# A first unit with a corrected plan: the first load in two halves, its transposes split with it, and the weight-sum stores tied to another event

## The chip, the cores and the metric

The kernel runs on one NeuronCore of a Trainium2 chip. The metric is the device time of one execution in microseconds (us); lower is better. The time of the kernel before is the median of three executions, and one more execution was profiled. All times in this document are in us unless they are marked ns.

## The reference

Six cross layers of a recommender network over a batch of 16384 rows of 1024 bf16 features. Each layer multiplies the running activation by a 1024x1024 weight matrix, adds a bias, multiplies element by element with the original input and adds the running activation:

```python
def reference(x0, ws, bs):          # x0: [16384, 1024]  ws: [6, 1024, 1024]  bs: [6, 1024]
    x = x0
    for l in range(6):
        proj = jnp.einsum('bd,de->be', x, ws[l]) + bs[l]
        x = x0 * proj + x
    return x
```

## The kernel before, in words

**Tiling.** The batch is cut into 16 pairs of 1024 rows (`PR`), and a unit is one pair in one layer, so there are 96 units. Two neighbouring pairs form a group and take turns: layer 0 of the first, layer 0 of the second, layer 1 of the first, and so on. The activations lie transposed in SBUF (features on the partitions): `x0T` holds the input of a pair and `xst` its running activation.

**Products.** A unit's matrix product is done by a Strassen-like scheme on 2x2 blocks. Seven block products, named 1 to 7, are formed from four input blocks, four combinations of input blocks (`T1` to `T4`, made on DVE) and eight weight blocks: four raw ones (`w12`, `1`, `2`, `4`) and four sums (`5`, `6`, `7`, `3`, made on DVE while the first pair passes, by the operations `c5`, `c6`, `c7`, `c3`). `P1.m` means product 1 for output block m: four matmuls of 128x512 (line 394). Most units carry the scheme one level deeper for some products (`5p1`, `2p3` and so on, line 588: four matmuls of 128x256); these need quarter sums of weights, which DVE writes into a third `xst` buffer. The very first unit uses no inner level: it is 28 groups `Pi.m` of four matmuls, and the transposes described next.

**PSUM.** There are eight banks, `pA0` to `pA3` and `pX0` to `pX3`. ACT copies a bank to another (`F1.m`, `F.m`) so that two products can go on from the same partial sum, and moves finished sums with their bias to SBUF (`E2.m`, `E4.m`, ...).

**The order.** All instructions are written out before the launch, one static order for each engine; engines wait for each other only through semaphores. The order of TensorE's work is a list of names written by hand for each kind of unit (`PE_FIRST` for the first). The orders of DVE, ACT, POOL and SP come from a planner (`schedule`), a list scheduler that knows an occupation (`occ`) and a latency (`lat`) for each operation and, for the start, a table `ARRIVE` of times at which loads are taken to have landed. The planner's start times also place the later weight loads on SP's queue (`plan_loads`, `pump`, line 315). A wrong entry in `ARRIVE` harms nothing by itself, but it can place an operation behind another one that in fact is ready later.

**The start.** DVE clears a tile, TensorE does eight dummy matmuls on it (line 770) and SP issues the loads in this order: `load_rows(0)`, 512 KB of x0 in row order (line 786); the weight block `1` (line 789); `load_rows(1)` and `load_rows(2)`; the weight block `2` (line 792); `w12` and `4` in halves (line 779); one block of x0 by a transposing DMA (line 796); and the four blocks of the second pair by transposing DMAs (line 418). The three blocks `rows[0..2]` are transposed by TensorE: the operation `ti.k` is four 128x128 matmuls against an identity (line 498) into one bank, which `ui.k` casts into `x0T` (line 502: k = 0, 2 on ACT, k = 1, 3 on DVE). `bT` transposes the bias (line 509), and two small DVE operations keep it.

**Stores of the weight sums.** The eight sums of a layer (four blocks, four tiles of quarter sums) are stored to DRAM from POOL's queue for the later groups (`save`, line 445, 512 KB each). In the first unit they stand behind `gate@0`, a one-column copy on POOL (line 722), which reads a block of `xst` that DVE writes by the operation `Qm`.

Of the kernel before, what the change touches and what calls it, by code (L numbers as in the profile page):

```python
# [14 lines left out]
IDENT = mybir.ActivationFunctionType.Identity  # L15

PE_FIRST = """
t0.0 t0.2 t0.3 t0.1 P1.2 t1.0 t1.1 P1.0 bT t1.3 t1.2 t2.0 t2.1 P2.0 t2.2 P1.1 t2.3 P2.1 P1.3 P2.2 P5.0 P5.1 P5.2 P2.3 P6.0 P6.3 P6.2 P5.3 P7.0 P6.1 P7.2 P3.0 P7.3 P4.2 P7.1 P3.3 P3.1 P4.1 P3.2 P4.3 P4.0
""".split()
PE_ONE_INNER = """  # L20
P1.1 P1.0 P1.3 P1.2 P2.1 P6.1 P2.0 P6.2 5p5 5p1 P2.2 P6.0 5p6 5p2 P6.3 P2.3 5p7 5p3 P7.2 P7.3 P3.3 5p4 P3.1 P7.1 P4.3
# [19 lines left out]
P1.1 P1.0 P6.1 P1.3 P1.2 P2.1 P2.0 P2.3 P6.2 P2.2 P5.3 P6.3 P5.2 P6.0 P5.1 P5.0 P3.3 P3.2 P3.1 P3.0 P7.0 P7.1 P7.3  # L41
P7.2 P4.0 P4.3 P4.1 P4.2 tV.1 tV.0 xW.1 xW.3 xW.0 tW.1 xW.2 tW.3 tW.2 tV.3 tV.2 tW.0
""".split()
ARRIVE = {"rows0": 5.0, "w0.1": 6.4, "rows1": 8.1, "rows2": 9.6, "w0.2": 11.1, "h0": 13.0, "h1": 14.6, "q": 16.6, "next": 20.6, "raw1": 34.2, "sums": 13.5}


ACCUM = (9.5, 12.0, 9.0)
# [144 lines left out]
def kernel(  # L192
# [7 lines left out]
    nc = tc.nc  # L200
    P = nc.NUM_PARTITIONS
# [3 lines left out]
    KH = KD // 2  # L205
    H = D // 2
    NB = 512
# [4 lines left out]
    KQ, HQ, NQ = KH // 2, H // 2, NB // 2  # L212
# [22 lines left out]
    P1s, P5s, Q, U, V, W, C3 = (work.tile([P, KH, KH, P], BF16, name=f"ev{i}") for i in range(7))  # L235
# [94 lines left out]
        return wt[(gl, w)]  # L330

    ops, named = [], {}
    FAR = 1e9

    def at_home(r):
        p, dot, m = r.partition(".")
        return home[p] + dot + m if p in home else r

    def op(name, eng, occ, lat, fn, rd=(), wr=(), weights=(), key=None, after=(), due=FAR, at=0.0):
        rd, wr = [at_home(r) for r in rd], [at_home(r) for r in wr]  # L340
        rd = tuple(rd) + tuple(slot[k] for k in weights if k in slot)
        for k in weights:
            uses_left[k] = uses_left.get(k, 0) + 1
        named[name] = len(ops)
        ops.append(Op(name, eng, occ, lat, fn, rd, tuple(wr), tuple(weights), key, tuple(named[a] for a in after), due, at))

    QD = ((0, 0), (0, 1), (1, 0), (1, 1))
    for u, (pr, l) in enumerate(units):
# [12 lines left out]
        x0T, xst = x0Ts[pr % 3], xsts[pr % 3]  # L361
# [10 lines left out]
        def pe(name, occ, fn, rd, wr, weights=(), u=u, gl=gl, line=line, at=0.0):  # L372
            op(f"{name}@{u}", "PE", occ, occ + 0.19, fn, rd, wr, [(gl, w) for w in weights], key=(u, line[name]), at=at)

        def act(name, fn, rd, wr, biased_=False, u=u, early=0.0):
            occ = 0.583 if biased_ else 0.482
            op(f"{name}@{u}", "ACT", occ, occ + 0.17 - early, fn, rd, wr)

        def dve(name, fn, n, rd, wr, weights=(), u=u, gl=gl, at=0.0, due=FAR, early=0.0):
            occ = n / 1920 + 0.068  # L380
            op(f"{name}@{u}", "DVE", occ, occ + 0.12 - early, fn, rd, wr, [(gl, w) for w in weights], at=at, due=due)
# [33 lines left out]
        def load(pt, q, at=0.0, after=(), u=u):  # L415
            def fn():
                r0 = pt * PR + q[1] * NB
                nc.sync.dma_start_transpose(out=blk(x0Ts[pt % 3], *q), in_=x0[r0:r0 + NB, q[0] * H:(q[0] + 1) * H])
            op(f"ld{q[0]}{q[1]}.{pt}@{u}", "SP", 3.0, 8.0, fn, [], [f"x0.{pt % 3}.{q[0]}{q[1]}"], at=at, after=after)

        def let(q, sp, u=u, xst=xst, grp=grp):
            def fn():
# [17 lines left out]
        if grp == 0 and lane == 0:  # L440
            raw = lambda w, gl=gl: wt[(gl, w)]

            def save(w, t, rd, weights=(), l=l, u=u, gl=gl):
                def fn():
                    nc.gpsimd.dma_start(Lc[l, CIDX[w]].rearrange("p (k e) -> p k e", k=KH), t())
                op(f"s{w}@{u}", "POOL", 1.0, 7.0, fn, rd + (["gate"] if u == 0 else []), (), [(gl, x) for x in weights])

            if first:
                ga = const.tile([P, 1], BF16, name="gate")

            def combo(w, a, b, o_, deps, gl=gl, raw=raw, first=first):
                def part(sl):
                    tt(raw(w)[:, :, sl], raw(a)[:, :, sl], raw(b)[:, :, sl], o_)

                def fn():
                    ring_make(gl, w)
                    part(slice(0, HQ) if w == "5" and first else slice(0, H))
                rd = [f"w{gl}.{d}" for d in deps]
                if w == "5" and first:
                    dve("c5", fn, KH * HQ, ["ringmake"], ["w0.5a", "ringmake", slot[gl, w]], [a, b], at=ARRIVE["h0"])  # L460
                    dve("c5b", lambda part=part: part(slice(HQ, H)), KH * HQ, ["w0.5a"], ["w0.5"], [a, b], at=ARRIVE["h1"])
                else:
                    dve("c" + w, fn, KH * H, rd + ["ringmake"], [f"w{gl}.{w}", "ringmake", slot[gl, w]], [a, b], at=ARRIVE["raw1"] if gl == 1 else 0.0)
            combo("5", "w12", "4", ADD, ())
            combo("6", "5", "1", SUB, ("5",))
            combo("7", "1", "w12", SUB, ())
            combo("3", "2", "6", SUB, ("6",))
            for Xi in ISLOT:
                if Xi == "4i" and l not in K4:
                    continue  # L470
                X = Xi[0]
                a = lambda r, c, X=X, gl=gl: wt[(gl, X)][:, r * KQ:(r + 1) * KQ, c * HQ:(c + 1) * HQ]
                sv = isum(Xi).rearrange("p q (k e) -> p q k e", k=KQ)
                src = [] if X == "2" else [f"w{gl}.{5 if X == '4' else X}"]
                nm = lambda i, Xi=Xi: f"is.{Xi}.{i}"

                def icombo(i, fn, rd, Xi=Xi, X=X, src=src, nm=nm):
                    dve(Xi + i, fn, KQ * HQ, [nm(r) for r in rd] + src, [nm(i), ISN[Xi]], [X], at=ARRIVE["sums"] if first else 0.0)
                icombo("5", lambda a=a, sv=sv: tt(sv[:, 0], a(0, 1), a(1, 1), ADD), ())
                icombo("6", lambda a=a, sv=sv: tt(sv[:, 1], sv[:, 0], a(0, 0), SUB), "5")  # L480
                icombo("3", lambda a=a, sv=sv: tt(sv[:, 2], a(1, 0), sv[:, 1], SUB), "6")
                icombo("7", lambda a=a, sv=sv: tt(sv[:, 3], a(0, 0), a(0, 1), SUB), ())
# [8 lines left out]
        if first:  # L491
            for i, (d, n) in enumerate(TURNED):
                for k in range(KH):
                    xb = k if i < 2 else 2 + k % 2

                    def turn(i=i, k=k, xb=xb):
                        for j in range(KH):
                            nc.tensor.matmul(pX[xb][:, j * P:(j + 1) * P], lhsT=rows[i][:, j, k, :], rhs=ident[:],  # L498
                                             start=(j == 0), stop=True, skip_group_check=True)
                    pe(f"t{i}.{k}", 0.25, turn, [], [Xn[xb]], at=ARRIVE[f"rows{i}"])  # L500
                    cp = nc.vector.tensor_copy if k % 2 else nc.scalar.copy
                    f = lambda cp=cp, d=d, n=n, k=k, xb=xb, x0T=x0T: cp(out=blk(x0T, d, n)[:, k], in_=pX[xb][:])  # L502
                    if k % 2:
                        dve(f"u{i}.{k}", f, 1024, [Xn[xb]], [Xn[xb], X0[d, n]], early=0.21 * k if i < 2 else 0.0)
                    else:
                        act(f"u{i}.{k}", f, [Xn[xb]], [Xn[xb], X0[d, n]], early=0.21 * k if i < 2 else 0.0)

            def turn_bias():
                nc.tensor.matmul(pA[KH - 1][:, 0:LK], lhsT=b_rows[:], rhs=ident[0:LK, 0:LK], start=True, stop=True, skip_group_check=True)
                nc.vector.tensor_scalar_add(b_all[:, 0:KD], pA[KH - 1][:, 0:KD], 1.0)  # L510
                nc.vector.tensor_copy(out=b_all[:, KD:LK], in_=pA[KH - 1][:, KD:LK])
            pe("bT", 0.1, turn_bias, [], [A[KH - 1], "bias"])
        ttop("T1", Tv[1], B12, B11, SUB, [XI[0, 1], XI[0, 0]], ["T1"])
        ttop("T2", Tv[2], B22, Tv[1], SUB, [XI[1, 1], "T1"], ["T2"], at=ARRIVE["q"] if first else 0.0)
        ttop("T3", Tv[3], B22, B12, SUB, [XI[1, 1], XI[0, 1]], ["T3"], at=ARRIVE["q"] if first else 0.0)
# [203 lines left out]

        if grp == 0 and lane == 0:  # L720
            if first:
                op("gate@0", "POOL", 0.1, 0.3, lambda ga=ga, xst=xst: nc.gpsimd.tensor_copy(ga[:], xst[:, 0, 0, 0, 0, 0:1]), [XO[0, 0]], ["gate"])
            for w in MADE:
                save(w, lambda w=w, gl=gl: wt[(gl, w)], [f"w{gl}.{w}"], [w])
            for Xi in ISLOT:
                if Xi == "4i" and l not in K4:
                    continue
                save(Xi, lambda Xi=Xi: isum(Xi), [f"is.{Xi}.{i}" for i in "5637"] + [ISN[Xi]])
# [52 lines left out]
    take(4)  # L781
    nc.scalar.dma_start(b_rows[:], bs.rearrange("l (m p) -> (l m) p", p=P))

    def load_rows(i):
        d, n = TURNED[i]
        nc.sync.dma_start(rows[i][:].rearrange("p j m r -> p j (m r)"), x0[n * NB:(n + 1) * NB, d * H:(d + 1) * H].rearrange("(j p) d -> p j d", p=P))

    load_rows(0)
    nc.sync.dma_start(wt[(0, "1")][:], w_src(0, "1"))
    load_rows(1)  # L790
    load_rows(2)
# [46 lines left out]
```

## Time and profile before

| | |
|---|---|
| median of 3 executions | 2209.33 (2209.17 to 2209.70) |
| profiled execution, its own time | 2209.77 |
| its span, first to last instruction | 2208.0 |
| PE busy | 2194.8 (99%), 14878 instructions |
| DVE busy | 2149.9 (97%) |
| ACT busy | 2055.4 (93%) |
| POOL busy | 255.1 (12%) |
| DMA | 512.30 MB, mean 232 GB/s |

PE is TensorE's matmul side and PEld its weight loads, DVE is VectorE, ACT is ScalarE, POOL is GpSimd, SP is SyncE; a "q" behind an engine's name marks its sequencer, which issues DMAs. The span is 1.8 shorter than the same execution's time, and that execution is 0.44 over the median. In a timeline line, the first number is when a run of like instructions starts, the second how long it lasts, and the bracket at its end tells how long the engine had been idle and who released it.

### The profile page before, as it was taken

Reading aid. Unit: us, or ns where it says so; the run is one execution under the profiler, and the core shown is the slowest. Engines: PE = TensorE matmul, PEld = TensorE weight load, DVE = VectorE, ACT = ScalarE, POOL = GpSimd, SP = SyncE. Lnnn points to the kernel's source line nnn. Section 1 sums busy time; section 2 is a strip of 40 time slices with the busy share of each in tenths; the row PEclk is TensorE's granted clock in tenths of the full one; section 3 lists DMA queues with packets and bytes.
Section 4 is the critical chain, followed back from the end, with each engine's and each line's share of the span. In section 5 each row is a group of like instructions: output and inputs, shape, how many; then the busy total and the mean of one; then the engine's idle time right before and its main releaser. Section 6 shows DMA issues by size and latency. Waiting matters only on the chain.

```text
span 2208.0 us, 40495 instructions
## 1 busy us (share of the span) xinstructions
PE 2194.8 (99%) x14878; PEld 1457.3 (66%) x14925; DVE 2149.9 (97%) x2583; ACT 2055.4 (93%) x3717; POOL 255.1 (12%) x325
## 2 busy tenths in 40 slices
PE   9999999999999999999999999999999999999998
PEld 5555566666666666666666666666666666666664
DVE  8999999999999999999999999999999999999997
ACT  7888899999999999999999999999999999999997
POOL 1122101111011110111001110011100111001110
PEclk9999999999999999999999999999999999999999
DMA  9689899988999889998999888998989989999897
GB/s 267 200 226 242 207 236 265 241 212 195 260 265 239 203 210 258 266 229 206 216 257 266 211 222 219 251 273 200 229 219 255 266 196 229 221 266 251 195 249 164
DMA packets 464424, 512.30 MB, mean 232 GB/s; under 512 B 270048, under 2 KB 383200, under 8 KB 464224
## 3 DMA queue, kind: packets, MB, share of 16 engines
q1 hardware_dynamic: 418352, 349.49, 55.7%
q0 software_dynamic: 44224, 159.41, 35.6%
q8 instruction: 117, 1.92, 0.3%
q10 hardware_dynamic: 1648, 0.80, 0.1%
q14 instruction: 83, 0.68, 0.1%
HBM read 252.72 MB, written 58.20 MB: 141 GB/s over the span
## 4 chain that ended last, share of the span: by engine, by line
PE 99%; DVE 0%; ACT 0%; issue 0%
PE pA L394 49%; PE pX L588 47%; PE pX L394 2%; PE pX L498 0%; DVE ti L266 0%; DVE T L266 0%; DVE xst L266 0%; PE pX L770 0%; ACT xst L704 0%; PE pA L770 0%; PE pA L694 0%; ACT ev L413 0%; DVE ev L266 0%; ACT x0T L502 0%; DVE x0T L502 0%
## 5 line engine op out<-in xcount | busy, mean ns | idle before, releaser
L588 PEld LDWEIGHTS <-wp 128*128 128x128 bf16 x7464 | 730.3, 98 | 231.2
L394 PE MATMUL pA<-T,wp 128*128 128x512 bf16 x3170 | 774.7, 379 | 1.6
L394 PEld LDWEIGHTS <-wp 128*128 128x128 bf16 x4768 | 466.4, 98 | 399.5 <-issue 1.4
L403 ACT CAST ev<-pX 128x512 bf16<-128x512 f32 x1144 | 648.6, 593 | 25.1 <-PE pX L588 21.9
L413 ACT ACTIVATE ev<-pA,b_all 128x512 bf16<-128x512 f32 x887 | 611.1, 693 | 38.9 <-PE pA L394 23.1
L588 PE MATMUL pX<-ti,wp 128*128 128x256 bf16 x4148 | 570.8, 273 | 0.0
L403 ACT COPY pX<-pX 128x512 f32<-128x512 f32 x678 | 388.2, 589 | 16.0 <-PE pX L588 11.8
L266 DVE TENSOR_TENSOR ev<-ev,ev 128x2048 bf16<-128x2048 bf16 (+1 forms) x282 | 339.8, 1212 | 13.6 <-ACT ev L413 6.0
L394 PE MATMUL pA<-xst,wp 128*128 128x512 bf16 x1056 | 260.7, 379 | 0.0
L413 ACT ACTIVATE xst<-pA,b_all 128x512 bf16<-128x512 f32 x324 | 222.2, 689 | 25.6 <-PE pA L394 15.7
L588 PE MATMUL pX<-xst,wp 128*128 128x256 bf16 x1512 | 226.8, 273 | 0.0
L266 DVE TENSOR_TENSOR ev<-ev,x0T 128x2048 bf16<-128x2048 bf16 (+2 forms) x188 | 223.5, 1194 | 2.0 <-ACT ev L413 1.8
L588 PE MATMUL pX<-T,wp 128*128 128x256 bf16 x1452 | 217.8, 273 | 0.0
L403 ACT CAST ip<-pX 128x512 bf16<-128x512 f32 x339 | 199.9, 591 | 2.8 <-PE pX L588 2.8
L266 DVE TENSOR_TENSOR T<-xst 128x2048 bf16<-128x2048 bf16 x160 | 194.8, 1218 | 2.0 <-PE pA L394 2.0
L266 DVE TENSOR_TENSOR T<-xst,T 128x2048 bf16<-128x2048 bf16 x160 | 194.9, 1218 | 0.1
L266 DVE TENSOR_TENSOR ev<-ev,ip 128x1024 bf16<-128x1024 bf16 x284 | 193.0, 684 | 0.4 <-ACT ev L403 0.4
L646 POOL DMA_DIRECT2D xst<-ev x144 | 124.3, 865 | 587.2 <-ACT pX L403 185.7
L588 PEld LDWEIGHTS <-x0T 128*128 128x128 bf16 x1596 | 156.2, 98 | 47.9
L266 DVE TENSOR_TENSOR xst<-xst,ev 128x2048 bf16<-128x2048 bf16 x136 | 166.0, 1221 | 13.3 <-ACT xst L403 6.5
L266 DVE TENSOR_TENSOR xst<-xst,x0T 128x2048 bf16<-128x2048 bf16 x136 | 165.8, 1219 | 0.7
L646 POOL DMA_DIRECT2D xst<-xst x112 | 96.2, 859 | 510.4 <-ACT ev L413 152.3
(72 smaller groups left out, 1825.2 us busy)
## 6 DMA issues: line engine op xcount, KB each, us to landing
wp<-Lc SPq DMA_DIRECT2D x280, 512.0 KB, 5.3
xst<-ev POOLq DMA_DIRECT2D x144, 512.0 KB, 5.6
wp<-in_ws_dram SPq DMA_DIRECT2D x120, 512.0 KB, 5.5
xst<-xst POOLq DMA_DIRECT2D x112, 512.0 KB, 7.7
out_dram<-x0T SPq DMA_DIRECT2D x60, 512.0 KB, 5.1
x0T<-Lc SPq DMA_DIRECT2D x49, 512.0 KB, 5.7
x0T<-in_ws_dram SPq DMA_DIRECT2D x28, 512.0 KB, 6.3
Lc<-wp POOLq DMA_DIRECT2D x24, 512.0 KB, 5.1
```

Source lines behind the costliest of these rows:

```text
L266: nc.vector.tensor_tensor(out=o, in0=a, in1=b, op=op)
L394: newest["pe"] = nc.tensor.matmul(o, lhsT=wt[(gl, w)][:, k, m * P:(m + 1) * P], rhs=r, start=(start and k == 0), stop=(k == KH - 1), skip_ ...
L403: act(name, lambda: nc.scalar.copy(out=dst, in_=src), rd, wr)
L413: act(name, lambda: nc.scalar.activation(out=dst, in_=src, func=IDENT, bias=b_all[:, c:c + 1], scale=1.0), rd + ["bias"], wr, True)
L588: newest["pe"] = nc.tensor.matmul(o if kmajor else o.rearrange("p (j r) -> p j r", r=P), lhsT=wv[:, k, m * P:(m + 1) * P], rhs=rhs(k), sta ...
L646: nc.gpsimd.dma_start(xblk(xst, *q), C[:], accum_op=ADD)
```

## The change

Five things are edited.

1. The first load, `load_rows(0)`, becomes two of 256 KB each. The operation `t0.k` becomes `t0.ka` and `t0.kb`, two transposes each, the first on the first half.
2. `PE_FIRST` is replaced: halves of `t0` first, then `bT`, and products `P1` and `P2` in another order among the transposes `t1` and `t2`.
3. `ARRIVE` has other times; the largest change is `next` (the blocks of the second pair), 20.6 before and 12.5 after, with an occupation of 2.1 instead of 3.0 for these four transposing loads. A store's latency is taken as 10.0 instead of 7.0.
4. The planner sees the quarters of a transposed block as resources of their own, and the two DVE operations behind `bT` become an operation of their own, `bC`.
5. `gate@0` reads a column of `W` that ACT writes by `E4.1`, instead of the block of `xst` that DVE writes by `Qm`.

```diff
 PE_FIRST = """
-t0.0 t0.2 t0.3 t0.1 P1.2 t1.0 t1.1 P1.0 bT t1.3 t1.2 t2.0 t2.1 P2.0 t2.2 P1.1 t2.3 P2.1 P1.3 P2.2 P5.0 P5.1 P5.2 P2.3 P6.0 P6.3 P6.2 P5.3 P7.0 P6.1 P7.2 P3.0 P7.3 P4.2 P7.1 P3.3 P3.1 P4.1 P3.2 P4.3 P4.0
+t0.1a t0.0a t0.2a t0.0b t0.1b t0.3a t0.2b t0.3b bT P1.0 P1.2 t1.0 t1.3 t1.2 t1.1 P1.1 t2.1 t2.0 P1.3 t2.3 t2.2 P2.0
+P2.1 P2.3 P2.2 P5.1 P5.0 P5.3 P5.2 P6.2 P6.3 P6.0 P6.1 P7.2 P3.0 P3.3 P7.0 P7.3 P7.1 P4.0 P3.1 P4.1 P4.2 P4.3 P3.2
 """.split()
-ARRIVE = {"rows0": 5.0, "w0.1": 6.4, "rows1": 8.1, "rows2": 9.6, "w0.2": 11.1, "h0": 13.0, "h1": 14.6, "q": 16.6, "next": 20.6, "raw1": 34.2, "sums": 13.5}
+ARRIVE = {"rows0a": 4.2, "rows0b": 4.9, "w0.1": 6.4, "rows1": 8.0, "rows2": 9.5, "w0.2": 11.1, "h0": 12.8, "h1": 14.5, "q": 16.6, "next": 12.5, "raw1": 33.8, "sums": 13.5}
...
+    pieces = {f"x0.0.{d}{n}" for d, n in TURNED}
...
+        rd += [f"{r}.{k}" for r in rd if r in pieces for k in range(KH)]
...
-            op(f"ld{q[0]}{q[1]}.{pt}@{u}", "SP", 3.0, 8.0, fn, [], [f"x0.{pt % 3}.{q[0]}{q[1]}"], at=at, after=after)
+            op(f"ld{q[0]}{q[1]}.{pt}@{u}", "SP", 2.1 if u == 1 else 3.0, 8.0, fn, [], [f"x0.{pt % 3}.{q[0]}{q[1]}"], at=at, after=after)
...
-                op(f"s{w}@{u}", "POOL", 1.0, 7.0, fn, rd + (["gate"] if u == 0 else []), (), [(gl, x) for x in weights])
+                op(f"s{w}@{u}", "POOL", 1.0, 10.0, fn, rd + (["gate"] if u == 0 else []), (), [(gl, x) for x in weights])
...
-                    def turn(i=i, k=k, xb=xb):
-                        for j in range(KH):
+                    def turn(js, i=i, k=k, xb=xb):
+                        for j in js:
...
-                    pe(f"t{i}.{k}", 0.25, turn, [], [Xn[xb]], at=ARRIVE[f"rows{i}"])
+                    if i:
+                        pe(f"t{i}.{k}", 0.25, lambda turn=turn: turn(range(KH)), [], [Xn[xb]], at=ARRIVE[f"rows{i}"])
+                    else:
+                        for h in range(2):
+                            pe(f"t0.{k}{'ab'[h]}", 0.21, lambda turn=turn, h=h: turn(range(h * KQ, (h + 1) * KQ)), [], [Xn[xb]], at=ARRIVE["rows0" + "ab"[h]])
...
-            pe("bT", 0.1, turn_bias, [], [A[KH - 1], "bias"])
+            pe("bT", 0.1, turn_bias, [], [A[KH - 1]])
+            dve("bC", keep_bias, 500, [A[KH - 1]], [A[KH - 1], "bias"])
...
-                op("gate@0", "POOL", 0.1, 0.3, lambda ga=ga, xst=xst: nc.gpsimd.tensor_copy(ga[:], xst[:, 0, 0, 0, 0, 0:1]), [XO[0, 0]], ["gate"])
+                op("gate@0", "POOL", 0.1, 0.3, lambda ga=ga, W=W: nc.gpsimd.tensor_copy(ga[:], W[:, 0, 1, 0:1]), ["W.1"], ["gate"])
...
-    load_rows(0)
+    load_rows(0, 0, KQ)
+    load_rows(0, KQ, KH)
     nc.sync.dma_start(wt[(0, "1")][:], w_src(0, "1"))
     load_rows(1)
     load_rows(2)
```

More of the change, by code (lines that the diff above doesn't have):

```diff
@@ L503, with keep_bias @@
                     if k % 2:
-                        dve(f"u{i}.{k}", f, 1024, [Xn[xb]], [Xn[xb], X0[d, n]], early=0.21 * k if i < 2 else 0.0)
+                        dve(f"u{i}.{k}", f, 1024, [Xn[xb]], [Xn[xb], f"{X0[d, n]}.{k}"], early=0.21 * k if i < 2 else 0.0)
                     else:
-                        act(f"u{i}.{k}", f, [Xn[xb]], [Xn[xb], X0[d, n]], early=0.21 * k if i < 2 else 0.0)
+                        act(f"u{i}.{k}", f, [Xn[xb]], [Xn[xb], f"{X0[d, n]}.{k}"], early=0.21 * k if i < 2 else 0.0)
             def turn_bias():
                 nc.tensor.matmul(pA[KH - 1][:, 0:LK], lhsT=b_rows[:], rhs=ident[0:LK, 0:LK], start=True, stop=True, skip_group_check=True)
+            def keep_bias():
                 nc.vector.tensor_scalar_add(b_all[:, 0:KD], pA[KH - 1][:, 0:KD], 1.0)
                 nc.vector.tensor_copy(out=b_all[:, KD:LK], in_=pA[KH - 1][:, KD:LK])
-            pe("bT", 0.1, turn_bias, [], [A[KH - 1], "bias"])
+            pe("bT", 0.1, turn_bias, [], [A[KH - 1]])
+            dve("bC", keep_bias, 500, [A[KH - 1]], [A[KH - 1], "bias"])
         ttop("T1", Tv[1], B12, B11, SUB, [XI[0, 1], XI[0, 0]], ["T1"])
@@ L782, with load_rows @@
     nc.scalar.dma_start(b_rows[:], bs.rearrange("l (m p) -> (l m) p", p=P))
-    def load_rows(i):
+    def load_rows(i, j0=0, j1=KH):
         d, n = TURNED[i]
-        nc.sync.dma_start(rows[i][:].rearrange("p j m r -> p j (m r)"), x0[n * NB:(n + 1) * NB, d * H:(d + 1) * H].rearrange("(j p) d -> p j d", p=P))
-    load_rows(0)
+        nc.sync.dma_start(rows[i][:, j0:j1].rearrange("p j m r -> p j (m r)"),
+                          x0[n * NB + j0 * P:n * NB + j1 * P, d * H:(d + 1) * H].rearrange("(j p) d -> p j d", p=P))
+    load_rows(0, 0, KQ)
+    load_rows(0, KQ, KH)
     nc.sync.dma_start(wt[(0, "1")][:], w_src(0, "1"))
```

## The prediction

> **What bounds the kernel now.** I read the page's busy times first, then TensorE's waits, then the timeline of the start, then the DMA issues one by one.
>
> ```profile
> PE 2194.8 (99%) x14878; PEld 1457.3 (66%) x14925; DVE 2149.9 (97%) x2583; ACT 2055.4 (93%) x3717; POOL 255.1 (12%) x325
> ```
> ```profile
> PE pX L770 <- DVE ti L767: 1.2, 1, 1.2
> PE pX L498 <- ACT x0T L502: 0.7, 1, 0.7
> PE pA L394 <- DVE x0T L502: 0.6, 1, 0.6
> PE pX L394 <- ACT pX L403: 0.4, 1, 0.4
> ```
>
> The first line gives busy time, share and instructions of each engine: TensorE is busy for all but 13.2 of the span. The second fence is the whole list of TensorE's waits, and all four lie before 14.3; from there to 2200 TensorE is never seen waiting. Some 8 of the 13.2 lie behind its last instruction. So whatever the change does elsewhere, it can gain only what the first 14.3 contain, unless a later order makes TensorE wait.
>
> ```profile
> 2.88 1.91 PE L770 MATMUL pA<-ti 128*128 128x512 bf16 x4
> 4.75 1.89 PE L498 MATMUL pX<-ident,ev 128*128 128x128 bf16 x16
> 6.44 0.43 PE L394 MATMUL pA<-x0T,wp 128*128 128x512 bf16 x1
> 7.42 0.97 PE L394 MATMUL pA<-x0T,wp 128*128 128x512 bf16 x3 [0.56 <-DVE x0T L502]
> ...
> 11.06 0.61 PE L498 MATMUL pX<-ident,ev 128*128 128x128 bf16 x8 [0.67 <-ACT x0T L502]
> ...
> 14.28 1.02 PE L394 MATMUL pX<-x0T,wp 128*128 128x512 bf16 x4 [0.43 <-ACT pX L403]
> 15.14 1.03 PE L394 MATMUL pA<-x0T,wp 128*128 128x512 bf16 x4
> 16.00 1.03 PE L394 MATMUL pX<-x0T,wp 128*128 128x512 bf16 x4
> 16.86 2.75 PE L394 MATMUL pX<-T,wp 128*128 128x512 bf16 x12
> ```
>
> Starts are the safe column (an end includes about 0.2 of pipeline). A product group takes 0.86 (15.14 to 16.00). A transpose takes 0.106 in the first block (4.75 to 6.44, sixteen) and 0.055 later (8.24 to 8.68, eight). Before 16.86, TensorE has done twelve `ti.k` and seven product groups: P1.0 to P1.3, P2.0, P2.1, P2.2.
>
> ```profile
> ev<-in_x_dram SPq DMA_DIRECT2D x1, 512.0 KB, 4.0
> wp<-in_ws_dram SPq DMA_DIRECT2D x1, 512.0 KB, 5.0
> ev<-in_x_dram SPq DMA_DIRECT2D x1, 512.0 KB, 5.9
> wp<-in_ws_dram SPq DMA_DIRECT2D x1, 256.0 KB, 8.1
> ```
>
> These are single issues; the last number is the time to landing. Added to the issue times of the timeline (0.75, 1.25, 1.80) the first block of x0 lands at 4.7, weight block 1 at 6.2, the second block at 7.7; by the same sums the third lands at 9.2, weight block 2 at 10.8, the halves of `w12` and `4` at 11.6, 12.5, 13.4 and 14.2, the transposed block at 16.4. One block each 1.5: the loads flow one behind the other.
>
> **The split load.** If 512 KB flow in 1.5, the first half lands near 3.95 and the second at 4.7. But the eight dummies run in order ahead of it: the last starts at 2.88 + 3 x 0.427 = 4.16 and gives TensorE free at 4.59. So the first transpose can start at 4.59 instead of 4.75: 0.16, and no more, from the landing. The rest of its worth is that the casts start sooner, below. The price: one more issue on SP (0.5, as the rows at 1.25 and 1.80) ahead of every load. SP's issues run seconds ahead of the flow (the third block is issued at 2.34 and lands at 9.2), so I take 0. The nearest rows of small transfers are the four 256 KB halves of weights: they land 0.9, 0.9 and 0.8 apart, against 0.75 for half of a 1.5 block, so a half may cost up to 0.15 more; two of them 0.3. I keep 0 to 0.3.
>
> The Trainium skill (DMA: Bandwidth & Descriptors, Anatomy of one DMA) gives each DMA about 2.0 fixed plus its bytes, and advises batches of 1 MiB and more. Here issues that overlap land 1.5 apart although each is 4 to 7 under way, so the trace shows the fixed part paid once; taken serially, the 2.0 of the Trainium skill would put every later load 2.0 back and leave 0.3 of the gain found below.
>
> **The first groups, step by step.** From 4.59: t0.1a, t0.0a, t0.2a take six transposes, to 5.23; t0.0b to 5.44, t0.1b to 5.66, t0.3a, t0.2b to 6.08, t0.3b to 6.30, `bT` to 6.4. A cast starts 0.24 behind the last transpose of its bank (6.44 to DVE's 6.68 in the timeline) and lasts 0.59 on ACT, 0.69 on DVE. So u0.0 is done at 6.27, u0.1 at 6.59, u0.2 at 6.91, u0.3 at 7.24. With 0.05 from cast to matmul (7.37 to 7.42), P1.0 has its four matmuls at 6.4, 6.64, 6.96 and 7.29 and is through at 7.5. Before, the fourth matmul of the first group started at 8.02: 0.73 gained, most of it because the DVE casts no longer wait for the last transposes (DVE's first cast at 6.68 becomes 5.90).
>
> Then, with landings as before: P1.2 to 8.37; t1 (landed 7.7), four times 0.22, to 9.26; P1.1 to 10.12; t2.1 and t2.0 (landed 9.2) to 10.57; P1.3 to 11.43; t2.3 and t2.2 to 11.87; the four P2 (weights landed 10.8) to 15.32. Each bank is free in time: the casts of t1 end near 10.3, t2.1's at 11.2 ahead of t2.3 at 11.43, F1.3 follows u2.3 near 13.1 ahead of P2.3 at 13.6. The waits of 0.67 and 0.43 go because P1 work, which needs only what has landed, stands where TensorE waited for casts and for weight block 2. Eight groups are done at 15.32; before, seven were at 16.86, and eight would be at 17.73. That is 2.41, less about 0.1 for hand-offs such as that at 11.72: **2.3**.
>
> **Does the next thing hold?** P5.1 at about 15.4 needs the first half of `c5` (second half-load lands at 12.5; DVE 0.69) and T1 (needs t2's casts, 12.6; 1.14 of DVE): DVE does both by 14.5. Spare 0.9. c5b (load lands 14.2) is through at 15.2, ahead of P5.3 at 17.1. P6.2 at 18.9 needs c6 and T2; T2 needs the block that lands at 16.4. DVE: c6 to 16.4, T2 to 17.6. Spare 1.3, or 0.1 should c7 go ahead of T2. T3, c7, c3 and T4 end by 22.3, ahead of P3.0 at 23.2. If this cover fails, TensorE waits for DVE for one 2048-element operation, 1.14.
>
> **The second unit.** This is the tight place, as DVE has no idle time from 30.73 to 160:
>
> ```profile
> 30.73 1.23 DVE L266 TENSOR_TENSOR ev<-ev,ev 128x2048 bf16<-128x2048 bf16 x1 [1.11 <-ACT ev L413]
> 31.88 1.22 DVE L266 TENSOR_TENSOR T<-x0T 128x2048 bf16<-128x2048 bf16 x1
> ```
> ```profile
> 34.90:160.00 125.10, 124.92 (x776) 75.94 (x777) 125.10 (x167) 108.82 (x193) 23.74 (x36) 1.00 0.76 221
> ```
>
> The windows line gives stretch, length, and busy time of PE, PEld, DVE, ACT and POOL: DVE is busy 125.10 of 125.10. If TensorE comes 2.3 sooner, DVE must too. It can: it idles 0.53 before the cast at 13.88, that cast itself (0.69) moves ahead of the weights' landing, and it idles 1.11 before 30.73 although T1 of the second pair, done only at 31.88, had its inputs at 20.1 and 21.8 (issues at 14.07 and 16.08 plus 6.0 and 5.7). Sum 2.33. The old plan took 20.6 + 8 = 28.6 for the first of these blocks, the new one 12.5 + 8 = 20.5, which fits what landed. So DVE gains what TensorE gains, with nothing over.
>
> **The gate.** Before, it ends POOL's wait at 29.35, then eight stores are issued to 33.96. E4.1 would follow P4.1, fourth from the end: the unit ends, by the timeline's first matmul of the next, at 34.99 - 2.3 = 32.7, so P4.1 at 30.1, E4.1 at 31.0, and gate and stores come 1.6 later than before. Queued behind it on POOL are only the eight stores; who waits for them is SP, on which every later weight load is queued:
>
> ```profile
> SPq L315 <- DMA Lc<-wp: 13.0, 1, 13.0
> SPq L315 <- PE pX L588: 6.1, 1, 6.1
> ```
>
> The first reload of a slot was held by a store for 13.0 and then for 6.1 by TensorE, to 45.86. With the store 1.6 later and TensorE 2.3 sooner, 2.2 of these 6.1 remain. Cost 0; without cover the reload is late by the difference, for weights first used in the fifth unit, past 100. Planner entries (10.0 for a store) issue nothing.
>
> **The sum.** 2209.77 of the profiled execution less 2.3 is 2207.5; less the 0.44 by which it is above the median, **2207.0**.
>
> **Rivals.**
> - *Part of it is given back* (gain 0.3 to 1.6, about 2208.4): DVE's 2.33 needs every gap closed; if the wait for an eviction like that at 30.73 stays, 1.11 of it goes and TensorE waits that much in the second unit. For it: the 125.10 of 125.10. Against it: TensorE never waited in that stretch, and the new plan knows the landings.
> - *The split does nothing*: the halves land no sooner or at 0.3 extra, and the casts start as before. Only the new order pays: 2.3 - 0.73 - 0.3 = 1.3, so 2208.0. Against it: the dummies end at 4.59 and casts only need their own bank.
> - *Each transfer pays its start by itself.* The first block needed 4.0, of which 1.5 is flow; if the second half added 2.5 to everything behind it, the gain would be -0.2: 2209.5. The 1.5 spacing speaks against it. The Trainium skill's fixed cost (DMA: Bandwidth & Descriptors, Anatomy of one DMA) is this rule.
> - *Slower: the new order places DVE work late.* All later start times move, and the planner's static order for DVE, ACT and SP moves with them. One 2048-element operation in front of a needed one makes TensorE wait 1.14, and in units 2 to 7 DVE has no idle to make it up. Two such eat the gain; six of them (6.8) give 2214 and pass 0.2%. For it: DVE at 100%. Against it: no wait in 2185 of span, so the old order had room, and most edits touch the first unit alone.
>
> **How the numbers follow.** 0.2%, 4.4, is about what a measurement of this kernel can tell from no change. Forecast (gain 1.6 to 2.8) 0.64; part given back 0.14; split useless 0.08; start paid again 0.02; slower, 0.09, of which 0.06 over 4.4; the rest, 0.03, a gain beyond 2.8. A gain of over 4.4 would need more than the waits that exist: 0.02 for an unseen cause. The range 2206.2 to 2209.2 takes in the forecast, the two partial cases with the 0.3 of the halves, and 0.2 at each end for the spread of the three executions (0.53). Faster by over 0.2% 0.02, same 0.92, slower 0.06.
>
> **What would show it.** First transpose at 4.6, P1.0's last matmul near 7.3, no TensorE wait over 0.3 after it, P5.1 starting at 15.3 to 15.5, second unit at 32.7, the gate near 31, first stores landing near 36, DVE's 1.1 wait near 30 gone. Wrong would be: weight block 1 landing after 6.5, a TensorE wait on DVE past 15, or a span that shrinks by less than the start of the second unit moved.

## The result and the profile after

The changed kernel takes 2218.66 (median of 5; 2217.03 to 2220.54) against 2209.55: ratio 1.0042, interval 1.0029 to 1.0056. It is 9.1 slower, where 2.3 faster was forecast. Its profiled execution took 2219.70, 1.04 above the median, with a span of 2217.9 against 2208.0.

Busy times and all of TensorE's waits, after:

```profile
PE 2197.4 (99%) x14877; PEld 1457.9 (66%) x14925; DVE 2150.1 (97%) x2583; ACT 2056.3 (93%) x3717; POOL 273.4 (12%) x325
```
```profile
PE pA L397 <- ACT ev L416: 4.1, 1, 4.1
PE pX L598 <- ACT pX L406: 3.2, 4, 1.7
PE pA L397 <- DMA wp<-in_ws_dram: 2.2, 1, 2.2
PE pX L780 <- DVE ti L777: 1.2, 1, 1.2
```

The three waits of the start that were to go (0.7, 0.6 and 0.4) are gone. In their place stands one wait of 2.2 for a weight load, and there are waits where there were none: 4.1 in one piece and 3.2 in four. POOL's busy time rose by 18.3 with the same 325 instructions.

Where the time is lost shows when the two traces are compared by ACT's 1267 evictions with bias (an eviction moves a finished sum from PSUM to SBUF), the start of the k-th in one against the k-th in the other. The changed kernel is 0.9 behind from the second unit, 0.6 near 80, 3.1 from 106 to 244, 8.7 from 310 to 1639, and 10.5 from 1775 to the last eviction. So there are four places: the start (0.9 lost instead of 2.3 gained), 89 to 106 (2.5), 268 (5.6), and 1678 to 1775 (1.8). Behind the last eviction 0.5 comes back.

**The start**, TensorE's timeline after, and the issues of the two halves and of weight block 1 (last number: time to landing):

```profile
4.59 1.35 PE L501 MATMUL pX<-ident,ev 128*128 128x128 bf16 x16
5.87 0.19 PE L516 MATMUL pA<-ident,b_rows 48*128 48x48 bf16 x1
8.23 3.26 PE L397 MATMUL pA<-x0T,wp 128*128 128x512 bf16 x8 [2.16 <-DMA wp<-in_ws_dram]
11.28 1.42 PE L501 MATMUL pX<-ident,ev 128*128 128x128 bf16 x16
...
35.88 0.60 PE L598 MATMUL pX<-ti,xst 128*128 128x256 bf16 x4
```
```profile
ev<-in_x_dram SPq DMA_DIRECT2D x1, 256.0 KB, 2.8
ev<-in_x_dram SPq DMA_DIRECT2D x1, 256.0 KB, 3.0
wp<-in_ws_dram SPq DMA_DIRECT2D x1, 512.0 KB, 6.4
```

The halves land early (issue plus time to landing: 0.75 + 2.8 = 3.6, 1.25 + 3.0 = 4.3) and the transposes start at 4.59 as forecast. But the weight block lands at 1.76 + 6.4 = 8.2, not 6.2. What flowed from 4 to 6, in the windows before and after (last column GB/s, ahead of it the DMA share):

```profile
4.00:6.00 2.00, 2.00 (x14) 1.25 (x13) 0.00 (x0) 0.60 (x2) 0.00 (x0) 1.00 1.07 365
```
```profile
4.00:6.00 2.00, 2.00 (x19) 1.42 (x17) 0.36 (x1) 0.47 (x1) 0.00 (x0) 1.00 0.48 136
```

The transfers behind the halves ran at 136 GB/s instead of 365, although the next three loads had been issued by 3.4. TensorE then waited 2.2, and its first eight matmuls took 3.05 (8.23 to 11.28), instead of 1.73: two at 0.23 and 0.27, then six at 0.427, which is half rate; the granted clock was 0.50 from 8.62 to 12.02. The Trainium skill (TensorE: Matmul & The Clock Gate, Part 1) says that the rate falls after an idle window of some 3.4 that runs free of the kernel; here 2.2 of idleness was enough. It is not enough each time: in the kernel with the old gate and in the one with one load (both below), a wait of 2.2 near 87 left the clock at 1.00.

**89 to 106.** The gate and the stores behind it, on POOL, and DVE after them:

```profile
34.24 17.85 POOL L732 COPY gate<-ev 128x1 bf16<-128x1 bf16 x1 [32.92 <-ACT ev L416]
52.02 1.74 POOL L448 DMA_DIRECT2D Lc<-xst  x3
```
```profile
50.82 1.22 DVE L267 TENSOR_TENSOR T<-xst,T 128x2048 bf16<-128x2048 bf16 x1
55.17 0.43 DVE L267 TENSOR_TENSOR xst<-wp 128x512 bf16<-128x512 bf16 x1 [3.13 <-DMA Lc<-xst]
```

The copy of one column started at 34.24, behind E4.1 (forecast: 31.0; the second unit starts at 35.88 instead of the forecast 32.7, 3.2 later), and lasted 17.85. It ended within 0.05 of the end of DVE's operation at 50.82. DVE stopped there because its next operation writes a tile whose store had not been issued: the store stood behind the gate. TensorE's waits near 89 and 100 (1.9 and 0.5 by the starts of its matmuls) follow from those 3.1, as the DMA gate below shows.

**268.** Issues of the accumulating transfers (POOL, `xst<-ev`: a DMA that adds what it carries to what lies there) and of weight loads (SP), before and then after, and the time to landing of the fourth transfer in each:

```profile
250.07 0.86 POOL L646 DMA_DIRECT2D xst<-ev  x1 [1.76 <-DVE ev L266]
250.78 0.37 SPq L315 DMA_DIRECT2D wp<-in_ws_dram  x1
251.25 2.45 SPq L315 DMA_DIRECT2D wp<-Lc  x3
xst<-ev POOLq DMA_DIRECT2D x1, 512.0 KB, 6.7
```
```profile
252.17 0.37 SPq L316 DMA_DIRECT2D wp<-in_ws_dram  x1
252.64 3.00 SPq L316 DMA_DIRECT2D wp<-Lc  x3
253.20 0.57 POOL L448 DMA_DIRECT2D Lc<-wp  x1 [1.42 <-DVE wp L267]
254.33 0.84 POOL L656 DMA_DIRECT2D xst<-ev  x1 [0.56 <-DVE ev L267]
xst<-ev POOLq DMA_DIRECT2D x1, 512.0 KB, 13.7
...
268.07 0.69 ACT L416 ACTIVATE ev<-pA,b_all 128x512 bf16<-128x512 f32 x1 [4.34 <-DMA xst<-ev]
268.81 3.17 PE L397 MATMUL pA<-T,wp 128*128 128x512 bf16 x8 [4.12 <-ACT ev L416]
```

Before, the transfer went out ahead of the loads; after, it goes out behind three of them (252.17, 252.64, 253.24) and a 512 KB store (253.20), with a fourth load 0.06 behind it, and lands at 268.0. ACT's eviction waits for it and TensorE for ACT, and TensorE's next eight matmuls take 3.0 instead of 1.7 (granted clock 0.50 from 268.03 to 271.44): by the starts 4.3 of standstill and 1.3, together 5.6, the largest piece of the loss.

### The profile page after: what moved, and what is told of

It is laid out like the page before. It is cut to its first block, busy times and chain, and to the rows that moved or that the text cites. A ratio compares the mean times of both kernels' runs of the same rounds, so it can differ in the third digit from the quotient of the medians.

```text
span 2217.9 us, 40494 instructions
## 1 busy us (share of the span) xinstructions
PE 2197.4 (99%) x14877; PEld 1457.9 (66%) x14925; DVE 2150.1 (97%) x2583; ACT 2056.3 (93%) x3717; POOL 273.4 (12%) x325
## 4 chain that ended last, share of the span: by engine, by line
PE 86%; DMA 1%; DVE 1%; issue 1%; ACT 0%; POOL 0%; ACTq 0%; POOLq 0%; DVEq 0%
PE pX L598 43%; PE pA L397 42%; DMA xst<-ev 1%; PE pX L397 1%; DMA x0T<-in_x_dram 0%; DVE xst L267 0%; DVE ev L267 0%; DVE ti L267 0%; DVE T L267 0%; ACT xst L714 0%; POOL xst L656 0%; PE pA L704 0%; ACT pX L406 0%; ACT ev L416 0%; POOL Lc L448 0%
```

## The experiments

The medians of the kernel before, measured again with each of the four sets of runs, were 2209.33, 2209.35, 2209.60 and 2209.21. Ratios are to those.

**The gate as before.**
```diff
-lambda ga=ga, W=W: nc.gpsimd.tensor_copy(ga[:], W[:, 0, 1, 0:1]), ["W.1"]
+lambda ga=ga, xst=xst: nc.gpsimd.tensor_copy(ga[:], xst[:, 0, 0, 0, 0, 0:1]), [XO[0, 0]]
```


> The changed kernel, with gate@0 reading the block of xst that Qm writes, as before the change. Theory: the gate's copy (17.85 us in the changed kernel, ended 0.05 after a DVE operation, just as the 0.32 us copy of before did) waits for a moment in which DVE runs nothing, whatever it reads. In the changed kernel Qm runs near 40 and DVE is busy without a break to 52.0, so the copy would start near 41 and still end at or after 50: no gain, 2217 to 2220. Rival (the new operand, or the earlier event, is at fault): the copy takes 0.3, stores start near 41, the wait of 3.1 of DVE and the TensorE waits of 1.9 and 0.5 near 89 and 100 go, and the time falls by 2 to 3 to about 2216.


Measured 2218.68, ratio 1.0045 [1.0028, 1.0062], as expected. The copy ran from 39.3 to 50.3. Undoing this part alone brings nothing, since the old event too now falls into DVE's unbroken stretch.

**The first load in one piece.**
```diff
-    load_rows(0, 0, KQ)
-    load_rows(0, KQ, KH)
+    load_rows(0)
```


> The changed kernel with its first load in one piece of 512 KB again; the transposes stay in halves in the same order. Theory: the two small transfers are why weight block 1 lands at 8.2 instead of 6.2. With one piece it lands at 6.2 again, the TensorE wait of 2.2 goes, the product groups behind it run at full rate, and the second unit starts near 32.8 instead of 35.9: 3 us less, about 2215.5, with the later waits as they are. Rival: the weight block is late for another reason (the run, or the memory), and lands near 8 here too: no change, 2218.7.


Measured 2218.58, ratio 1.0042 [1.0027, 1.0057]. The profile did what the theory said: weight block at 6.2, no long wait, second unit at 32.81, 2.18 ahead of the kernel before. But the gate's copy took 18.5, and by eviction times 2.9 were lost near 89 to 104, 5.9 near 266 and 2.1 later. The median did not fall. So in this trace the start is repaired, and the gain does not reach the end; a miss for the forecast of the time. Its profiled execution (2218.53) lies at its median and that of the changed kernel 1.04 above, so the 3.1 between the two starts need not be the difference of typical executions.

**The gate as a small DMA.**
```diff
-lambda ga=ga, W=W: nc.gpsimd.tensor_copy(ga[:], W[:, 0, 1, 0:1])
+lambda ga=ga, W=W: nc.gpsimd.dma_start(ga[:], W[0:1, 0, 1, 0:32])
```


> The changed kernel, with the gate as a DMA of 64 bytes issued by POOL that reads the same row of W behind the same E4.1, instead of a copy on POOL's compute side. Theory (the copy is shut out by DVE): the gate is through at 35, stores are issued from 35 to 40 and land from 40 to 50, DVE's wait of 3.1 at 52 goes and with it the TensorE waits near 89 (1.9) and 100 (0.5): 2.0 to 2.5 less, about 2216.3; the 4.3 near 268 may stay. Rival (the long bar of POOL is only its rough record, and the stores wait for something else): the first store is still issued near 52 and the time stays at 2218.7.


Measured 2216.04, ratio 1.0029 [1.0017, 1.0041]. POOL's timeline:

```profile
34.22 0.65 POOL L732 DMA_DIRECT2D gate<-ev  x1 [32.90 <-ACT ev L416]
34.86 1.60 POOL L448 DMA_DIRECT2D Lc<-xst  x3
```

Same event, same 34.2, and now 0.65 under the same DVE load. DVE's 3.1 and TensorE's waits near 89 and 100 are gone, 2.6 in the median. In the new order the copy on POOL's compute side was the cause, not the event. The wait near 268 stayed (3.9), so it does not come from the late stores.

**Both.** The edits of the last two.


> Both edits, the gate as a small DMA and the first load in one piece. If the two causes are separate, their gains add: 5 to 5.5 less than the changed kernel, 2213 to 2214, and what is left over the kernel before is the wait of 4.3 near 268 (an accumulating transfer behind weight loads) and the 1.5 near 1680. If the late transfers near 250 follow from the late stores, that wait goes too and the time is about 2208, below the kernel before.


Measured 2214.15, ratio 1.0022 [1.0012, 1.0031], 1.9 less than with the DMA gate alone. Up to 245 this kernel is 2.2 ahead of the kernel before; then it loses 7.0 near 264 (4.5 of waiting by the starts, the rest half rate). The forecast of 2.3 for the start holds in this trace once the two causes ahead of 245 are away.

**The split load alone, in the kernel before.**
```diff
-    load_rows(0)
+    load_rows(0, 0, KQ)
+    load_rows(0, KQ, KH)
```


> The kernel before, with its first load sent as two halves of 256 KB and nothing else changed (the transposes t0.k stay whole, the order and the plan are those of before). Theory: behind two half loads the weight block 1 lands 0.8 to 2 late (7.0 to 8.2; it was at 7.1, 7.9 and 8.2 in the kernels with two halves, 6.2 to 6.6 in those with one piece), and every load behind it as well, so the start is 1 to 2 later and, as nothing later has slack to give back, so is the end: 2210.3 to 2211.5. Rival: the late landing needs the rest of the change too: 2209.3.


Measured 2210.18, ratio 1.0005 [0.9996, 1.0014], not clear of no change and just under the expected 2210.3 to 2211.5. In the profile (an execution of 2212.39) weight block 1 landed at 8.1, with a wait of 1.6 and 2.85 lost. The ten times lie apart: five at 2209.4 to 2209.9, one at 2210.5, four at 2211.3 to 2212.5. The late landing needs nothing but the split; by these times it seems not to hit every execution, but only one was profiled.

**The new gate alone, in the kernel before.** The line of the change, nothing else.


> The kernel before with the new gate alone: POOL's copy reads the column of W that E4.1 writes. Theory: E4.1 ends near 33.3, and DVE is busy without a gap from 30.73, so the copy waits for DVE's next stop, which is the first quarter-sum write of the second layer near 51 that needs a stored buffer: copy to about 51, first store landing near 54, DVE waits about 3, TensorE waits about 2.4 near 90 to 100: 2211.5 to 2212. Rival (the gate costs only in the new order): 2209.3.


Measured 2209.35, ratio 0.9999 [0.9990, 1.0009]. A miss: 2211.5 to 2212 was expected. The copy ran from 33.65 to 34.58, until 0.05 after the end of the one DVE operation then running. So the new event shows no cost in the old order.

**The order near the end of the first group.** The list that the planner writes, compared by name, has `c3` of unit 10 (a weight sum) one place ahead of `Um` of unit 9 on DVE; before, `5t2` of unit 10 (a small sum of inputs) stood in that place and `c3` after `Um`. `Um` multiplies a finished block by x0, and the fourth accumulating transfer carries its result. DVE before and after, with `Um` as `ev<-ev,x0T` and `c3` as `wp<-wp,wp`:

```profile
248.56 1.22 DVE L266 TENSOR_TENSOR ev<-ev,x0T 128x2048 bf16<-128x2048 bf16 x1
249.69 1.22 DVE L266 TENSOR_TENSOR wp<-wp,wp 128x2048 bf16<-128x2048 bf16 x1
```
```profile
251.68 1.22 DVE L267 TENSOR_TENSOR wp<-wp,wp 128x2048 bf16<-128x2048 bf16 x1
252.82 1.22 DVE L267 TENSOR_TENSOR ev<-ev,x0T 128x2048 bf16<-128x2048 bf16 x1
```

On top of the gate as a DMA and the load in one piece, one more edge holds `c3` behind `Um`:
```diff
+        after = tuple(after) + (("Um@9",) if name == "c3@10" else ())
         named[name] = len(ops)
```


> The kernel with the DMA gate and the single first load, and one more edge for the planner: c3 of the last layer (unit 10) may not be placed ahead of Um of unit 9, as in the order of the kernel before. Theory: with c3 ahead of Um, the fourth accumulating transfer of unit 9 is issued 1.1 later, and the weight loads whose slot c3 frees are issued 1.7 sooner against TensorE, so the transfer queues behind 2 MB of loads and lands after 13.9 instead of 6.7; TensorE waits 4.5 near 264 and then runs eight matmuls at half rate (7.0 in all). With the edge the transfer is issued ahead of the loads, the wait goes, and the time is 2214.15 - 7.0 = 2207.2, about 2.1 below the kernel before. Rival: the loads are early because of their planned issue (239.1 instead of 243.8 for one of them), not because of c3; then the transfer is still caught, and the time stays near 2213 to 2214.


Measured 2208.85, ratio 0.9997 [0.9989, 1.0006]; 5.3 less than without the edge, where 7.0 (to 2207.2) was expected. The issues are in their old order:

```profile
248.35 0.87 POOL L657 DMA_DIRECT2D xst<-ev  x1 [1.74 <-DVE ev L267]
249.59 0.37 SPq L316 DMA_DIRECT2D wp<-in_ws_dram  x1
```

TensorE's wait near 264 is gone. The order of one pair of operations on DVE was worth 5.3 in the median.

**The same edge in the changed kernel.**


> The changed kernel with that one edge alone; the split load and the copy as a gate stay. Theory (the three causes add): 5.6 less than the changed kernel, about 2213.0, and what is left over the kernel before is the late weight block (+0.6 to 0.9 at the second unit) and the late stores (+2.4 near 100). Rival (the wait near 268 comes from the late stores): it stays, 2218.7.


Measured 2212.51, ratio 1.0013 [1.0004, 1.0022]: 6.2 less than the changed kernel, with 2.2 near 88 as the largest wait left. Here the clock did fall behind that wait (0.50 from 89.1 to 92.5). This cause adds to the other two: the edge takes away 6.2 with them and 5.3 without.

**Two halves, with the other two causes away.**


> The changed kernel with the DMA gate and the edge that keeps c3 behind Um; of the three causes only the split load is left. Theory: weight block 1 lands 0.5 to 2 later than with one piece, by a different amount in each execution; TensorE waits for it, 1 to 2, and its first groups then run at half rate in some executions. Against the kernel with one piece (2208.85): 0.8 to 1.5 more, 2209.7 to 2210.3, with a spread of 3. Rival (the late landing in the profiles is a chance of the profiled executions): 2208.6 to 2208.9.


This has the DMA gate and the edge; only the split is left. Measured 2209.64, ratio 1.0000 [0.9991, 1.0009], 2207.95 to 2210.76; in the profile the weight block landed at 7.5, and TensorE waited 1.6. Against one piece (2208.85) it is 0.8 more, 0.5 when each is set against its own kernel before; with these intervals that is not clear of zero.

**Two halves, weight block 1 from ACT.** On top of the last:
```diff
+    nc.scalar.dma_start(wt[(0, "1")][:], w_src(0, "1"))
...
-    nc.sync.dma_start(wt[(0, "1")][:], w_src(0, "1"))
```


> The same, but weight block 1 is issued by ACT, behind the small bias load, instead of by SP behind the two halves. Theory A (SP's queue hands the weight block out slowly behind two small transfers): it flows beside the halves and lands by 6.4; halves near 4.6; no wait, 2208.3 to 2208.7, below the one-piece kernel. Theory B (whatever flows between 4 and 6 is slow, in any queue): it lands after 7 here too, and the time is that of the two halves, about 2210.


Measured 2208.66, ratio 0.9996 [0.9987, 1.0005]. The weight block landed at 6.0, and the hole in the flow is gone:

```profile
4.00:6.00 2.00, 2.00 (x19) 1.37 (x17) 0.40 (x1) 0.51 (x2) 0.00 (x0) 1.00 1.06 360
...
6.13 2.06 PE L398 MATMUL pA<-x0T,wp 128*128 128x512 bf16 x8
```

By eviction times it is 2.45 ahead at the second unit and 2.65 at 1494; near 1666 and 1689 it loses 1.0. It speaks for theory A: the hole belongs to SP's queue behind two small transfers, not to the memory at that time. The DMA view from 4 to 5, by queue (packets, MB, share of 16 engines; q10 carries the block from ACT, q1 is SP's), fits it: the flow is ACT's, and SP's queue moves next to nothing, with three more loads issued on it by 2.8. As ACT's block keeps the engines full, it is no proof by itself:

```profile
q10 hardware_dynamic: 350, 0.36, 103.7%
q1 hardware_dynamic: 18, 0.01, 4.0%
```

Ten of its eleven executions (2207.48 to 2208.94) lie below the lowest of the 27 of the kernel before in the same set (2209.05); the eleventh took 2212.01. So a gain of some 0.9 is likely, though the interval of the ratio takes in 1.

**One piece, weight block 1 from ACT.**


> One piece of 512 KB for the first load, DMA gate, c3 behind Um, and weight block 1 issued by ACT. The two transfers then share the flow: both theories expect the first block near 5.5 to 6 instead of 4.7 to 5.3 and the weight block near 6.3, so the start is 0.5 to 1 later than with SP alone: 2209.3 to 2209.8.


Measured 2211.10, ratio 1.0005 [0.9996, 1.0014]. A miss in size (2209.3 to 2209.8 was expected): the weight block landed at 8.5, while the second and third blocks of x0 landed at 7.0 and 9.2, so it shared the flow with three blocks. TensorE waited 2.6 and then ran at half rate for long; the windows' granted clock (third figure from the end) shows it:

```profile
8.00:14.00 6.00, 5.30 (x24) 3.05 (x26) 0.80 (x2) 1.12 (x3) 0.00 (x0) 0.50 1.19 308
```

**The gate's copy later still, in the kernel before.** As the new gate, but with `W[:, 0, 0, 0:1]` and `["W.0"]`.


> The kernel before with the gate's copy tied to E4.0, TensorE's last group of the first unit, so that it starts near 36, 2.4 later than with E4.1 (33.7, where the copy took 0.9). If the copy only has to wait for the end of the DVE operation that is running, it takes up to 1.2 again, stores start near 37 and the time is 2209.3 to 2209.6. If it is shut out for as long as DVE runs operations of two inputs without a stop, as in the four kernels of the changed order (11.0 to 18.5), it ends near 51, when DVE stops for a store that has not landed; DVE then waits 3, TensorE about 2.4 near 90 to 100, and the time is 2211.5 to 2212.


Measured 2209.28, ratio 1.0000 [0.9990, 1.0009]. The copy ran from 36.08 to 36.75, again to 0.05 after the end of a DVE operation (36.02 to 36.70), though DVE went on without a stop. Being late under a busy DVE is thus not enough to shut the copy out.

## Why the prediction was wrong

The forecast's sum had one term, the 2.3 of the start, and took three others as 0. Between the profiles the split load cost 3.1 (0.9 behind instead of 2.2 ahead with one piece), the gate 2.5 and the changed order 5.6; another 1.8 near 1666 to 1775 is not explained.

- **"I take 0" for the split load** was mis-sized, and its upper end of 0.3 with it. In the six profiles of kernels with two halves and weight block 1 all on SP the block landed at 7.1 to 8.2, in the six with one piece at 6.2 to 6.8: 0.3 to 2.0 later. The four half loads that I took as the nearest row stood behind five other loads; the trace of before has no small loads at the head of the queue. In medians the split costs 1.9 with the DMA gate, 0.1 with the copy gate, and 0.8 in the kernel before and in the kernel without the other causes, which the intervals do not separate from 0.
- **The rival "each transfer pays its start by itself"** (2.5 for the second half) is not what happened: the halves landed 0.7 apart, and it was the load behind them that came late, by 2.0 in the changed kernel.
- **"The gate. Cost 0"** failed on what it takes without saying so: that the gate takes 0.3 wherever it stands. I moved its time but not its cover. It failed too where it says who waits for the stores (SP): DVE waited 3.1 for one of them. The 0.32 copy of before ended 0.05 after a DVE operation with an idle 1.1 behind it. In four kernels of the new order the copy took 11.0 to 18.5, until DVE stopped. The Trainium skill (SBUF — State Buffer, Who interferes with whom) says that a DVE operation with two SBUF inputs and a GpSimd instruction that reads SBUF exclude each other for a whole instruction, and infers that descriptor generation, which a DMA from POOL needs, takes the write side of their shared ports, which such a DVE operation leaves free; the DMA gate's 0.65 agrees. In the trace the copy stayed shut out over 23 DVE operations on end.
- **The rival "slower: the new order places DVE work late"** named the right mechanism, and I gave it 0.09. I looked for it in units 2 to 7 as DVE's backlog and priced a misplaced operation at 1.14. The one that mattered sat in units 9 and 10, and its price was 5.6 to 7.0 in the traces (5.3 and 6.2 in the medians), because it put one accumulating transfer behind three weight loads and a store. "Most edits touch the first unit alone" was the wrong argument: the planner fills each hole with what is ready, and DVE's order changed in units up to 12 and in later groups. Which of the planner's edits turned that pair (the new times, or the store's 10.0) no run separates.
- **"That is 2.41, less about 0.1"** was right. With weight block 1 landing at 6.0 to 6.8, the start came out 1.8 to 2.2 ahead (one piece) and 2.45 (block 1 from ACT). (The "seconds" by which SP's issues run ahead are microseconds.)
- **"Does the next thing hold"** and **"The second unit"** held: no TensorE wait over 0.6 from 10 to 85 in any kernel of the new order, and DVE's 1.1 near 30 is gone. The worth of that is what the other two causes then spent.

What stays open: why the transfers behind two small ones are slow on SP's queue in some executions; what let the copy through in the order of before; the 0.2 to 1.8 that the new order loses near 1666 to 1775 (DVE there waits 0.8 to 2.3 for a block of x0 in six traces), and 0.5 to 1.1 more between 1940 and 2000 in four; and why the one-piece load brought nothing to the median while the copy gate was in. By their intervals the two best versions measured, 2208.66 and 2208.85, are not told from the kernel before; forecast was 2207.0.

## What to carry to other kernels

Where the time after the start has no slack shown, a gain at the start is kept only if every later order stays the same; compare the planned orders of all queues, name by name, before trusting it, and look where an accumulating transfer and a burst of loads are issued within some 2 us of each other. A tiny compute operation used as a gate on POOL can be held up for as long as DVE runs without a stop (0.3 to 18.5 here); a DMA of a few bytes on the same queue waited for the same event and took 0.65. A load split for an earlier first byte needs a look at the transfer behind it, not only at its own halves.

## What was not expected of the hardware

- Two transfers of 256 KB at the head of SP's queue had landed by 4.4, one of 512 KB at 4.7 to 5.3, but from 4 to 6 the flow was 136 to 275 GB/s in the six profiles with two, against 322 to 371 with one. With the next block on ACT's queue the rate was 360.
- A POOL copy of 128x1 took 17.85 beside an unbroken run of DVE operations, and a POOL DMA of 64 bytes 0.65 in the same place.
- A 512 KB accumulating transfer issued behind three weight loads and a store landed after 13.7, ahead of them after 6.7.
- A TensorE wait of 2.2 was followed by matmuls at half rate, so that the second unit came 3.2 later than forecast; one of 2.6 was followed by six microseconds at a granted clock of 0.50. Waits of one length went both ways: 2.2 near 87 left the clock at 1.00 in two kernels and was followed by 0.50 in a third, and 1.6 at the start was followed by 0.50 in one kernel of two.
